# Gated attention on one core: two query blocks per load of K and V

## The chip, the cores and the metric

The kernel runs on one core of one Trainium2 chip. The metric is the device time of one execution in microseconds (us); several runs are taken and the median is given. A profile is one further execution, recorded instruction by instruction.

The core has five instruction streams. PE multiplies matrices (its weight loads, PEld, are listed apart). ACT evaluates functions such as exp. DVE and POOL do elementwise work and sums. SP issues most of the DMA transfers. PE writes to PSUM, the others read it; each stream runs its own instructions in order and waits on semaphores for the others.

## The reference

There are 2048 rows of width 512, and 32 heads of 128 channels with 2048 cached keys each. The output is an input plus attention times a gate.

```
x  = A_x;  xn = layernorm(x)
q  = (xn @ wq) as 32 heads of 128
p  = softmax(q @ k_cache^T * 128**-0.5)
s  = (p @ v_cache) @ wo
h  = relu(xn @ w1 + b1) ** 2           # 1792 wide
g  = silu(h @ w2 + b2)
out = x + s * g
```

## The kernel before

**Blocks, units, steps.** The 2048 query rows are cut into four blocks of 512 (`NQB`, `QB`). A unit `g` is one head for one block; before, unit `g` is block `g // 32`, head `g % 32`, so all heads of block 0 come first, then all of block 1, and so on: 128 units. A unit has eight steps (`NPR`), each for 256 keys; 1024 steps in all (`NPAIR`). In a step PE makes scores for two tiles of 128 keys (`gen_scores`, two matmuls of 512 columns into psA), ACT turns them into exponentials in one instruction of 128x1024 into one of eight buffers of pT, and PE, two steps later (`LAG`), multiplies the exponentials with V (`gen_pv`) into psO.

**Two ways for a unit.** Most units are "B" units (`gen_pv_b`): V is the stationary operand, 16 matmuls of 512 columns. The softmax denominators are then summed apart: POOL adds the halves of a pT tile into h_sum (`part_add`), DVE reduces it (`part_half`), or DVE reduces the pT tile alone (`den_part`); the sums go through DRAM (d_scr, r_scr) and come back spread over all partitions (r_all), and POOL scales the output into oT (`den_scale`). The units in `A_SET`, 20 of them, go the "A" way (`gen_pv`): the exponentials are stationary, V has a column of ones added, and 64 matmuls of 129 columns give output and denominators together. DVE copies them out (o_un), POOL scales (`norm_scale`), and a transposing DMA writes oT (`gen_oT`).

**K, V and weights.** K is loaded by two transposing DMAs and V by four plain ones per unit (`fill_k`, `fill_v`), into rings of three (`NSL`), two units ahead. `wq_sb` holds query weights per head in a ring of four. W1 and W2 stay in SBUF for the whole kernel (both are named w_sb in the profile). `wo_all` holds 16 heads of wo and is filled anew for every block.

**Projections.** In block 0, a head's Q is made from four matmuls of 512 columns (`job_proj`) and one cast by DVE to qt_sb. From block 1 on, heads come in pairs and are projected by seven products rather than eight (`job_pair`): 14 matmuls of 256 columns, whose stationary operands are sums of weight blocks made ahead (`wp_mul` on ACT, `wp_sums` on POOL, stored to wq_scr and loaded by `fill_pair`) and whose moving operands are sums of x blocks in xs_t (`x_sum` on POOL). DVE puts the seven results together (u_t and qt_sb, seven instructions of 128x256). The weights are scaled first by a power of two per head (`head_max`, `chunk_scale`).

**The gate and the output.** `job_h` makes h for a block, 14 chunks of four matmuls; DVE takes relu plus bias (r_t) and multiplies (h2T). `job_o2` makes 14 matmuls for each of four row tiles; tanh on ACT and two products on POOL give the gate in g_all. `job_wo` multiplies oT with wo in chunks of eight heads (the last of the last block has 16), and sums in acc; `acc_gate`, `acc_add` and `finish` apply the gate, add x and write out.

**The order.** A planner in Python writes the order of every engine by hand. `_Sched` keeps a modelled clock for each engine and `emit` adds an instruction with its waits. The main loop goes over the 1024 steps: scores of this step, then filler matmuls (`fill_one`: projections, h, o2, wo), then the values of two steps before. `credit` hands the fillers out evenly over the steps that are left; `soon` lets a filler in only if its inputs are ready by the modelled clock. Work for DVE, POOL and SP waits in lists (`quiet`, `pool_quiet`, `sync_quiet`) with due times. Before the loop the first head is written out by hand; its K is transposed by PE, and `fill_k(1)` waits for that (`t_kT0`). At the end a tail multiplies the last 16 heads with wo, 14 matmuls inside the loop and 22 (`n_after`) behind it, ahead of the ones that need the last head.

Nearly every instruction is made by a helper, so one line of the profile stands for many uses: 259 and 264 are matmuls, 268 ACT, 272, 277, 278, 282, 286 elementwise work, 327 the transposing sum, 335 and 339 plain and transposing DMAs.

Of the kernel before, what the change touches and what calls it, by code (L numbers as in the profile page):

```python
# [12 lines left out]
P = 128  # L13
# [48 lines left out]
def _cost(name, fn):  # L62
# [15 lines left out]
    if f in (_reduce_t, _abs_max):  # L78
        n = _elements(k["in_"])
    elif f is _reduce:  # L80
        n = _elements(k["in_"]) * 1.3 + 35
    elif f is _recip:
        n = n * 3.1
    elif f in (_bn_stats,):
        n = _elements(k["in_"])
    elif f is _ts and _in_sbuf(k["in0"]):
        n = n / 2
    elif f is _tt and k["out"].dtype == F16:
        n = n / 2
# [252 lines left out]
def bass_recurrent_scan__mha_block_cached__dense_activation_squared_relu__prompt_kernel(  # L342
# [17 lines left out]
    QB = 512  # L360
# [10 lines left out]
    SPB = H * NPR  # L371
    HC = 8
    NCH = H // HC
    CH = [[(m * HC, (m + 1) * HC) for m in range(NCH)] for _ in range(NQB - 1)]
    CH.append([(0, HC), (HC, 2 * HC), (2 * HC, H)])
# [9 lines left out]
    A_SET = (0, 10, 20, 28, 32, 36, 42, 44, 50, 60, 63, 72, 78, 84, 94, 102, 120, 125, 126, 127)  # L385
# [7 lines left out]
    NRW = 2 * HC  # L393
    WQ_PACE = 20
    WQ_FIRST = 64
    POOL_OWED = 1000
    HALF_SLACK = 300
    VW = 136

# [14 lines left out]
    NSL, NSW, NQS, NPT, NOT, NOC, NHS = 3, 4, 5, 8, 21, 5, 3  # L414
    xnT = sb("xnT", [P, NDC, 2 * QB], BF16)
    w1_sb = sb("w1_sb", [P, NDC, F], BF16)
# [4 lines left out]
    oT = sb("oT", [P, NOT, QB], BF16)  # L421
    acc = sb("acc", [P, TPB, D], F32)
# [10 lines left out]
    xs_t = sb("xs_t", [P, 4, 2, HB], F16)  # L433
# [23 lines left out]
    r_all = sb("r_all", [P, 2, QB], F32)  # L457
    d_scr = nc.dram_tensor("d_scr", [2, P, 32], F32, kind="Internal").ap()
# [43 lines left out]
    sl_xl = [S.slot(f"xl{i}") for i in range(TPB)]  # L502
    sl_xT = [S.slot(f"xT{i}") for i in range(TPB)]
    sl_w1 = [S.slot(f"w1{i}") for i in range(NFC // 2)]
# [20 lines left out]

    def is_b(g):
        assert g in b_no or g in a_no
        return g in b_no
# [17 lines left out]
    for i in [x for x in range(NSL) if at_a(x)]:  # L546
# [7 lines left out]
    t_xuse = {}  # L554
    n_xuse = [2] + [0] * (NQB - 1)
# [4 lines left out]

    def ln_x(jt):
        return x_t[:, jt - 2, :] if 2 <= jt < TPB else x_ln[:, jt % 2, :]

    def ln_y(jt):
        return out_t[:, jt - 2, :] if 2 <= jt < TPB else xn_t[:, jt % 2, :]

    def ln_prev(jt):
        return jt - TPB if jt < TPB + 2 else jt - 2

    def ln_load(j, i, eng=SP):  # L570
        jt = j * TPB + i
        assert jt < TPB or ln_prev(jt) in t_xn
        t_xl[jt] = S.emit_dma(
            eng, partial(_dma, out=ln_x(jt), in_=A_x[0, jt * P:(jt + 1) * P, :]), sl_xl[i],
# [24 lines left out]
    def ln_scale(j, i):  # L599
        jt = j * TPB + i  # L600
        assert jt < TPB or ln_prev(jt) in t_xnr
# [5 lines left out]
    def ln_transpose(j, i):  # L607
        jt = j * TPB + i
        t_xnr[jt] = tok_xT[j][i] = S.emit_dma(
            SP, partial(_dmaT, out=xnT[:, :, jt % (2 * TPB) * P:(jt % (2 * TPB) + 1) * P],  # L610
                        in_=ln_y(jt)),
            sl_xT[i], deps=[t_xn[jt], t_xuse.get(j - 2)])
        assert j < 2 or n_xuse[j - 2] == NFC + (H if j == 2 else NPP)

    def ln_next(j, i):
        ln_scale(j, i)
        ln_transpose(j, i)
        if i + 2 < TPB:
# [8 lines left out]
    def load_k0(b):  # L627
# [3 lines left out]
            SP, partial(_dma, out=kT[:, NSL - 1, b * n * P:(b + 1) * n * P],  # L631
# [14 lines left out]
    def k0_transpose(b):  # L646
        n = NKT // 2
        for c in range(n):
            t_kT0[b] = E(PE, partial(_peT, out=bankO(b).bitcast(BF16)[:, c * P:(c + 1) * P],
                                     in_=kT[:, NSL - 1, (b * n + c) * P:(b * n + c + 1) * P],  # L650
# [61 lines left out]
    t_kfill = [None] * NG  # L712
    t_vfill = [None] * NG
    t_wqfill = [None] * NG
# [13 lines left out]
    def fill_k(g, part=None):  # L728
        if g >= NG:
            return  # L730
        h, i, prev = g % H, g % NSL, g - NSL
        n = Sk // NKP
        for x in range(NKP) if part is None else [part]:
            t_kfill[g] = S.emit_dma(
                SP, partial(_dmaT, out=kT[:, i, x * n:(x + 1) * n],
                            in_=A_k_cache[0, h, x * n:(x + 1) * n, :]),
                sl_k[i], deps=[t_S_last[prev] if prev >= 0 else t_kT0[1]],
                group_done=x == NKP - 1)

    def fill_v(g, part=None):  # L740
        if g >= NG:
            return
        h, i, prev = g % H, g % NSL, g - NSL
        n = NKT // NVP
        dst = v_sb[:, i, :, 0:Dh] if at_a(g) else v_row[:, i]
        if part == 2 and at_a(g):
            t_ones[g] = E(GP, partial(_memset, out=v_sb[:, i, :, Dh:Dh + 1], val=1.0),
                          deps=[t_PV_last[prev]])
        for x in range(NVP) if part is None else [part]:
            t_vfill[g] = S.emit_dma(  # L750
# [3 lines left out]
                sl_v[i], deps=[t_PV_last[prev] if prev >= 0 else None],  # L754
                group_done=x == NVP - 1)

    def fill_wq(g, eng=SP):
        if g >= H:
            return
        h, i, prev = g % H, g % NSW, g - NSW  # L760
        t_wqfill[g] = S.emit_dma(
            eng, partial(_dma, out=wq_sb[:, i, :, :],
                        in_=A_wq[:, h * Dh:(h + 1) * Dh].rearrange("(c p) e -> p c e", p=P)),
            sl_wq[i], deps=[t_proj[prev], t_hm[prev]] if prev >= 0 else [])

    def wo_prev(j, i):
        h = i * HC + HC - 1
        return (j * H + h - NRW) if h >= NRW else (j - 1) * H + h + NRW

    def load_wo(j, i, x):  # L770
        n = HC // NWP
        h0 = i * HC + x * n
        prev = wo_prev(j, i)
        tok_wo[j, i] = S.emit_dma(
            SP, partial(_dma, out=wo_all[:, h0 % NRW:h0 % NRW + n, :], in_=wo_view[:, h0:h0 + n, :]),
            sl_wo[i % 2], deps=[t_wodone[prev]] if prev >= 0 else [], group_done=x == NWP - 1)
# [12 lines left out]
    t_xs = {0: None}  # L789
# [4 lines left out]
    def wp_load(p):  # L794
        t_wn[p] = S.emit_dma(
            SP, partial(_dma, out=wq_new[:, 0:2 * NDC * Dh].rearrange("p (c e) -> p c e", c=NDC),
                        in_=A_wq[:, 2 * p * Dh:(2 * p + 2) * Dh].rearrange("(c p) e -> p c e", p=P)),
            sl_wn, deps=[t_ws.get(p - 1)])
# [7 lines left out]

    def chunk_turn(q):
        t_mr[q] = E(DV, partial(_transpose32, out=mx_r[:], in_=mx_q[:]),
                    deps=list(t_hm.values()) + [t_mp.get(q - 1)])
# [1159 lines left out]
```

## Time and profile before

| | us |
|---|---|
| median of 3 runs (1211.37 to 1211.56) | 1211.52 |
| span of the profiled execution | 1210.6 |
| DMA: moved, mean rate | 235.79 MB, 195 GB/s |
| exponentials on ACT, 1025 instructions | 1028.6 |
| halves added on POOL (h_sum), 666 | 754.1 |
| DVE sums of h_sum, 666, and of pT, 198 | 442.8 and 238.3 |
| pair evictions on DVE: u_t, qt_sb, 144 each, at 0.458 and 0.465; 48 at 0.452 | 65.9, 66.9, 21.7 |
| relu on DVE (r_t), 56 at 0.723 | 40.5 |
| oT scaled on POOL, 108 at 1.283 | 138.5 |
| a DMA issued by POOL: 16 of x_t at 0.593 | 9.5 |

The span is the time from the first to the last recorded instruction of one execution. Busy times are unions over an engine's instructions, so a share of 99% means that the engine is hardly ever without an instruction; a matmul record includes the time that its result takes through the array, and records overlap. "x" gives the number of instructions, "<-" what a group writes and reads, and behind the bar stand the busy time and the mean time of one in ns, then idle time ahead of the group and what ended it.

### The profile page before, as it was taken

The numbers are of one execution on the slowest core, as the hardware profiler recorded it, in microseconds if no ns is written. First come the engines' busy times: TensorE is split into PE (matmuls) and PEld (weight loads), VectorE is DVE, ScalarE is ACT, GpSimd is POOL, SyncE is SP. The second block draws the span as 40 slices with busy tenths as digits, with TensorE's granted clock in tenths as the row PEclk, the third lists the DMA queues.
The fourth block names the chain that finished last, engine by engine and source line by source line (L and its number), as shares of the span: only waits on it lengthen the run. The fifth ranks groups of instructions, "written<-read, shape, count | busy, mean of one in ns | idle before, by whom it ended". The sixth has DMA issues, their size and how long they took to land.

```text
span 1210.6 us, 21032 instructions
## 1 busy us (share of the span) xinstructions
PE 1198.5 (99%) x6858; PEld 711.4 (59%) x6989; DVE 1076.3 (89%) x2037; ACT 1095.4 (90%) x1185; POOL 1078.1 (89%) x1035
## 2 busy tenths in 40 slices
PE   9999999999999999999999999999999999999999
PEld 7555555556665665555655656565565655555666
DVE  6999998998989987998799999978979999999873
ACT  7998999999999999999899899989999999999994
POOL 5998998999889888999899897979989899999873
PEclk9999999999999999999999999999999999999999
DMA  9889988999998999898968888986787887878972
GB/s 210 185 206 209 220 199 207 207 196 225 218 215 210 232 226 204 200 216 196 209 169 200 189 195 194 191 199 166 181 212 164 196 194 172 202 178 187 201 162 49
DMA packets 505821, 235.79 MB, mean 195 GB/s; under 512 B 394704, under 2 KB 482512, under 8 KB 505712
## 3 DMA queue, kind: packets, MB, share of 16 engines
q1 hardware_dynamic: 503616, 230.38, 84.8%
q0 software_dynamic: 1424, 3.81, 1.0%
q8 instruction: 55, 0.90, 0.3%
q14 instruction: 54, 0.44, 0.1%
q10 hardware_dynamic: 672, 0.26, 0.1%
HBM read 152.06 MB, written 11.49 MB: 135 GB/s over the span
## 4 chain that ended last, share of the span: by engine, by line
PE 90%; DVE 4%; POOL 3%; issue 1%; DMA 1%; ACT 1%; SPq 0%; POOLq 0%; ACTq 0%; DVEq 0%
PE psA L259 33%; PE psO L259 28%; PE psF L259 17%; PE psO L264 5%; PE psF L264 5%; POOL h_sum L272 2%; DVE d_part L327 2%; POOL oT L272 1%; DMA r_all<-r_scr 1%; DMA kT<-in_A_k_cache_dram 0%; DVE h2T L282 0%; DVE u_t L277 0%; ACT pT L268 0%; DVE r_t L278 0%; DVE qt_sb L282 0%
## 5 line engine op out<-in xcount | busy, mean ns | idle before, releaser
L268 ACT ACTIVATE pT<-psA 128x1024 bf16<-128x1024 f32 x1025 | 1028.6, 1025 | 95.1 <-PE psA L259 67.5
L272 POOL TENSOR_TENSOR h_sum<-pT 128x512 f32<-128x512 bf16 x666 | 754.1, 1158 | 47.9 <-ACT pT L268 34.7
L259 PE MATMUL psA<-qt_sb,kT 128*128 128x512 bf16 x1969 | 592.1, 380 | 4.0 <-ACT pT L268 0.3
L259 PE MATMUL psO<-pT,v_sb 128*128 128x512 bf16 x1683 | 504.2, 379 | 2.8 <-DVE o_un L286 0.3
L327 DVE TRANSPOSE_TENSOR_REDUCE d_part<-h_sum 128x16 f32<-128x512 f32 x666 | 442.8, 683 | 16.4 <-POOL h_sum L272 15.2
L259 PEld LDWEIGHTS psA<-qt_sb,kT 128*128 128x128 bf16 x2032 | 279.3, 145 | 166.0 <-ACT pT L268 8.3
L259 PEld LDWEIGHTS psO<-pT,v_sb 128*128 128x128 bf16 x1728 | 168.9, 98 | 152.8 <-issue 1.8
L327 DVE TRANSPOSE_TENSOR_REDUCE d_part<-pT 128x32 f32<-128x1024 bf16 x198 | 238.3, 1211 | 2.3 <-ACT pT L268 2.0
L259 PE MATMUL psF<-wo_all,oT 128*128 128x512 bf16 x468 | 153.1, 379 | 0.5
L272 POOL TENSOR_TENSOR oT<-o_col,r_all 128x512 bf16<-128x512 f32 x108 | 138.5, 1283 | 10.9 <-DMA r_all<-r_scr 10.7
L264 PEld LDWEIGHTS psO<-v_sb,pT 128*128 128x128 bf16 x1280 | 85.3, 98 | 30.8 <-issue 0.4
L264 PE MATMUL psO<-v_sb,pT 128*128 128x129 bf16 x1280 | 98.3, 220 | 0.1
L259 PE MATMUL psF<-w_sb,h2T 128*128 128x512 bf16 x220 | 73.1, 379 | 0.2
L259 PE MATMUL psF<-xnT,w_sb 128*128 128x512 bf16 x218 | 72.2, 379 | 0.3
L282 DVE SCALAR_TENSOR_TENSOR qt_sb<-psF,sc_q,u_t 128x256 bf16<-128x256 f32 x144 | 66.9, 465 | 5.1 <-PE psF L264 3.0
L277 DVE TENSOR_SCALAR u_t<-psF,sc_q 128x256 f32<-128x256 f32 x144 | 65.9, 458 | 6.1 <-PE psF L264 5.2
L259 PEld LDWEIGHTS psF<-wo_all,oT 128*128 128x128 bf16 x480 | 46.9, 98 | 41.2
L264 PE MATMUL psF<-xs_t,wq_sb 128*128 128x256 f16 x384 | 68.3, 273 | 0.0
L268 ACT ACTIVATE o_col<-psO 128x512 f32<-128x512 f32 x108 | 64.2, 594 | 0.0
L264 PEld LDWEIGHTS psF<-xs_t,wq_sb 128*128 128x128 f16 (+1 forms) x384 | 37.1, 98 | 29.2 <-DVE u_t L277 2.6
L264 PE MATMUL psF<-xnT,wq_sb 128*128 128x256 bf16 x288 | 54.2, 273 | 0.0
L272 POOL TENSOR_TENSOR wq_sb<-wq_sb 128x256 f16<-128x256 bf16 (+1 forms) x64 | 42.9, 673 | 11.5 <-ACT wq_sb L268 11.3
(86 smaller groups left out, 724.6 us busy)
## 6 DMA issues: line engine op xcount, KB each, us to landing
v_sb<-in_A_v_cache_dram SPq DMA_DIRECT2D x508, 128.0 KB, 2.9
r_all<-r_scr SPq DMA_DIRECT2D x108, 256.0 KB, 3.9
wq_sb<-wq_scr SPq DMA_DIRECT2D x48, 448.0 KB, 4.3
wo_all<-in_A_wo_dram SPq DMA_DIRECT2D x64, 256.0 KB, 3.4
wq_scr<-wq_sb SPq DMA_DIRECT2D x16, 448.0 KB, 3.7
wq_sb<-in_A_wq_dram SPq DMA_DIRECT2D x16, 256.0 KB, 4.3
kT<-in_A_k_cache_dram SPq DMA_TRANSPOSE x254, 3.9
wq_sb<-in_A_wq_dram SPq DMA_DIRECT2D x31, 128.0 KB, 3.1
```

Of the source, the lines that this page charges most:

```text
L259: return e.matmul(out, lhsT, rhs, start=start, stop=stop)
L264: return e.matmul(out, lhsT, rhs, start=start, stop=stop, skip_group_check=True)
L268: return e.activation(out, in_, func, bias=bias, scale=scale)
L272: return e.tensor_tensor(out, in0, in1, op)
L277: return e.tensor_scalar(out, in0, scalar1=scalar1, scalar2=None, op0=op0)
L282: return e.scalar_tensor_tensor(out=out, in0=in0, scalar=scalar, in1=in1, op0=op0, op1=op1)
L327: return e.tensor_reduce(out, in_, axis=AX.X, op=ALU.add, apply_transpose=True)
```

## The change

**Order of units.** Blocks are taken two at a time. For a pair of blocks, heads go two by two, and the units run (block a, head h), (block b, head h), (block a, head h+1), (block b, head h+1); the first and the last two heads of the whole run as (a, h), (a, h+1), (b, h), (b, h+1). `kv_of(g)` numbers the 64 loads of K and V, each used by two units; the rings have two places rather than three. K of head 0, transposed by PE, is now read through oT's memory, and the load of head 1 waits no more for its transposes.

```diff
+    for jj in range(NQB // 2):
+        for h in range(0, H, 2):
+            a, b = [(2 * jj, h), (2 * jj, h + 1)], [(2 * jj + 1, h), (2 * jj + 1, h + 1)]
+            ends = (jj, h) in ((0, 0), (NQB // 2 - 1, H - 2))
+            units += a + b if ends else [a[0], b[0], a[1], b[1]]
-    NSL, NSW, NQS, NPT, NOT, NOC, NHS = 3, 4, 5, 8, 21, 5, 3
+    NSL, NSW, NQS, NPT, NOC, NHS = 2, 4, 6, 8, 5, 3
-    A_SET = (0, 10, 20, 28, 32, 36, 42, 44, 50, 60, 63, 72, 78, 84, 94, 102, 120, 125, 126, 127)
+    A_SET = (0, 3, 6, 9, 13, 15, 19, 20, 26, 30, 32, 45, 50, 54, 62, 71, 75, 78, 101, 109, 118, 125, 126, 127)
```

**Block 1 early.** xnT holds all four blocks. The four row tiles of block 1 are loaded ahead of head 1's K, into memory that acc uses later, and normalised right behind the first head's hand-written part; blocks 2 and 3 come from step 138 on.

```diff
+    for i in range(TPB):
+        ln_load(1, i)
     fill_k(1)
-    fill_wq(2)
     fill_v(1)
...
+    for i in range(TPB):
+        ln_bn(1, i)
+        ln_rstd(1, i)
+    for i in range(TPB):
+        calm(1, partial(ln_next, 1, i))
```

**Projections.** Only heads 0 to 7 of blocks 0 and 1 are projected plainly: 16 units rather than 32, two of them in the hand-written start. All others go in pairs, 56 rather than 48. A pair's weights are loaded once for two blocks (28 loads of wq_scr). `PREP` sets the order in which weights are made ready: the maxima of heads 8 to 31 come from loads of their own (`pair_max`), and the weights of heads 0 to 7 are prepared late, for blocks 2 and 3. xs_t has a place for each of two blocks.

```diff
-    for g in range(2, H):
-        jobs.append((NPR * g - 15, NPR * (g - 2), job_proj(g), g))
-    for g in range(H, NG, 2):
-        jobs.append((NPR * g - 20, NPR * g - 26, job_pair(g), g))
+    for g in range(2, 4 * NPL):
+        jobs.append((NPR * g - 15, NPR * (g - 3), job_proj(g), ("q", g)))
     for j in range(NQB):
+        for p in range(NPL if j < 2 else 0, NPP):
+            g = un[j, 2 * p]
+            jobs.append((NPR * g - 40, NPR * g - 26, job_pair(j, p), ("pair", j, p)))
```

**W1, wo and gates.** W1 is streamed through three places of 256 columns, seven loads for each block. wo_all holds eight heads and is filled once for two blocks; its last chunk goes into W2's memory. The gates are written to DRAM (g_scr) by POOL's queue and loaded by SP when a block's output needs them. acc has eight row tiles.

```diff
+        def gate():
+            t = E(GP, partial(_tt, out=th_t[:, 0, :], in0=th_t[:, 0, :], in1=z_t[:, s, :],
+                              op=ALU.mult), deps=[box[0]])
+            t_gated[jt] = t_zrd[s] = t_thr[0] = E(
+                GP, partial(_tt, out=out_t[:, s, :], in0=th_t[:, 0, :], in1=z_t[:, s, :],
+                            op=ALU.add), deps=[t, t_outdma[s]])
+            t_gw[jt] = t_outdma[s] = S.emit_dma(
+                GP, partial(_dma, out=g_scr[jt], in_=out_t[:, s, :]), sl_out[s],
+                deps=[t_gated[jt]])
```

**Relu and the last sums.** The relu of h goes to ACT where the model has ACT idle, and otherwise stays on DVE. `finish` always runs on DVE and is used for blocks 2 and 3 only; for blocks 0 and 1 all four chunks are summed in acc, and `acc_add` writes the output tile.

```diff
-            t1 = E(DV, partial(_ts, out=r_t[:, s, :], in0=bankF(bank), scalar1=b1f[:, c:c + 1],
-                               scalar2=0.0, op0=ALU.add, op1=ALU.max),
-                   deps=[box[0], t_b1[0], t_rt[s]])
+            deps = [box[0], t_b1[0], t_rt[s]]
+            if AC.t <= PE.t + ACT_ROOM:
+                t1 = E(AC, partial(_act, out=r_t[:, s, :], in_=bankF(bank), func=ACT.Relu,
+                                   bias=b1f[:, c:c + 1]), deps=deps)
+            else:
+                t1 = E(DV, partial(_ts, out=r_t[:, s, :], in0=bankF(bank), scalar1=b1f[:, c:c + 1],
+                                   scalar2=0.0, op0=ALU.add, op1=ALU.max), deps=deps)
```

**The planner.** `job_needs` lists what each filler waits for. `crowded` holds back fillers without a due time while projections with a near one are outstanding, and `need_q`, called at the first step of a unit, places fillers until the unit's Q has been placed.

```diff
+    def crowded(n, step):
+        for key, rel, job, tag in jobs[:8]:
+            if deadline(tag) is not None:
+                n += job[0]
+                if deadline(tag) < step + 4 + n * 0.8:
+                    return True
+        return False
+
+    def need_q(g, step):
+        room = ROOM
+        while t_evac[g] is None:
+            if fill_one(step) or fill_one(step, any_job=True):
+                continue
...
+        if k == 0 and pi >= NPR:
+            need_q(g, pi)
         if pi >= NPR:
             gen_scores(pi)
```

**The end.** The last chunk has eight heads; block 2's last chunk (32 matmuls) and block 3's (the tail) run behind the last scores, block 2's first.

More of the change, by code (lines that the diff above doesn't have):

```diff
@@ L87, in _cost @@
         n = n / 2
-    elif f is _tt and k["out"].dtype == F16:
+    elif f is _tt and k["out"].dtype in (F16, BF16) and k["in0"].dtype in (F16, BF16):
         n = n / 2
@@ L524, in at_a, with wide @@
         return g in A_SET
+    def wide(kv):
+        return any(at_a(g) for g in range(NG) if kv_of(g) == kv)
     def is_b(g):
@@ L872, in wp_sums @@
+    def wp_sums(n, i):
         a, s = parts(wq_new)
[L873 to L877 removed]
```

721 lines of the change are left out of this document (418 added, 303 removed).

## Prediction

> **What bounds the kernel now.** I read four views in this order: the busy times and the chain of waits on the page, the stretches of 40 us, the waits of PE, and the time line of the end.
>
> ```profile
> span 1210.6 us, 21032 instructions
> PE 1198.5 (99%) x6858; PEld 711.4 (59%) x6989; DVE 1076.3 (89%) x2037; ACT 1095.4 (90%) x1185; POOL 1078.1 (89%) x1035
> PEclk9999999999999999999999999999999999999999
> PE 90%; DVE 4%; POOL 3%; issue 1%; DMA 1%; ACT 1%; SPq 0%; POOLq 0%; ACTq 0%; DVEq 0%
> ...
> L259 PE MATMUL psA<-qt_sb,kT 128*128 128x512 bf16 x1969 | 592.1, 380 | 4.0 <-ACT pT L268 0.3
> L264 PE MATMUL psO<-v_sb,pT 128*128 128x129 bf16 x1280 | 98.3, 220 | 0.1
> L264 PE MATMUL psF<-xs_t,wq_sb 128*128 128x256 f16 x384 | 68.3, 273 | 0.0
> ```
>
> PE is in use all the time and is nine tenths of the chain. The other three engines have 115 to 134 us of idle time each, so they matter only where they make PE wait.
>
> ```profile
> 0.00:40.00 40.00, 38.18 (x328) 26.89 (x332) 29.09 (x60) 31.26 (x34) 24.73 (x36) 1.00 1.06 208
> 40.00:80.00 40.00, 39.79 (x183) 21.33 (x186) 39.16 (x75) 36.95 (x40) 37.22 (x35) 1.00 0.82 185
> 480.00:520.00 40.00, 39.48 (x226) 23.58 (x228) 33.26 (x61) 38.15 (x43) 34.59 (x36) 1.00 0.95 212
> 800.00:840.00 40.00, 39.53 (x201) 22.57 (x203) 35.63 (x68) 36.54 (x41) 39.06 (x35) 1.00 0.86 209
> ```
>
> Columns are the stretch, its length, busy time and count of PE, PEld, DVE, ACT and POOL, granted clock, DMA share, GB/s. The second stretch has 186 weight loads, one for each matmul of 512 columns: 40/186 = 0.215 us from one to the next. I take 0.216. A matmul of 256 columns is 380 - 273 = 107 ns shorter, so 0.109 us; one of 129 columns 160 ns shorter, so 0.056 to 0.057 us. The time line gives the same: 16 of 129 columns in 1.07 us, whose last has 0.22 us of latency, 0.85/15 = 0.057.
>
> Now the budget. The weight loads are complete; 131 matmul records are missing (6989 - 6858), and each hole looks like 2 x 216 - 379 = 53 ns of idle time. The weight loads by group give 4824 of 512 columns, 688 of 256, 1280 of 129 and 195 of 128 (0.056): 1042.0 + 75.0 + 72.9 + 10.9 us, and 1.8 us because the first 36 run at half rate (4.02 us for 36). That is **1202.6 us of matmul issue in a span of 1210.6**. Of the 8 us left, 1.0 is ahead of the first matmul, 2.6 behind the last. Full stretches read 39.79 (four holes); what the stretches from 40 to 1200 lack of that adds up to 1.5 us, the largest being the 0.31 and 0.26 shown. The rest is in the first 16 us. So no wait worth more than 1.5 us is there to be removed in the body.
>
> ```profile
> PE psO L303 <- DMA kT<-in_A_k_cache_dram: 0.5, 1, 0.5
> ...
> 1195.11 1.07 PE L264 MATMUL psO<-v_sb,pT 128*128 128x129 bf16 x16
> 1197.12 3.40 PE L259 MATMUL psF<-wo_all,oT 128*128 128x512 bf16 x15
> ```
>
> The only wait of PE for a DMA is 0.5 us, at the start.
>
> **The change part by part.** *Traffic.* A unit's K and V are four loads of 128 KB and two of 256 KB, 1 MB; 64 of 128 go: -64 MB. wo is loaded 32 times, not 64, at 256 KB: -8. Pair weights 28, not 48, at 448 KB: -8.8. W1 28, not 7, at 256 KB: +5.3. Gates, 16 writes and 16 reads at 128 KB: +4. Net some -71 MB of 236. The DMA engines are at 0.82 to 1.06 in the stretches above, but PE waited for them 0.5 us in all: **0 us**. What hides it is PE's own queue of work. The SP queue is shorter too (a K half holds it 1.2 us), so what moves past it, pair weights and wo, comes no later.
>
> *Projections.* 14 plain ones stay in the stream where there were 30: 64 fewer matmuls of 512, -13.8 us. Eight more pairs: 112 matmuls of 256, +12.2. **-1.6 us.**
>
> *Heads.* 24 heads, not 20, go the A way: four times (64 x 0.057 - 16 x 0.216) = 4 x 0.19 = **+0.8 us**. Other engines: four B heads take 32 denominators with them (by the shares of the 666 and 198: -28.6 us on POOL, -25.8 on DVE), 4 x 1.05 of sums, turns and reciprocals on DVE, 4 x 1.28 on POOL; four A heads give back 4.1 and 4.2.
>
> *Other engines' ledger.* A pair's evictions are seven instructions, 3 x 0.458 + 3 x 0.465 + 0.452 = 3.2 us of DVE; eight more are +25.8, less 16 casts at 0.62 = -9.9. The last sums all go to DVE (+7 x 1.26), accumulator adds +12 x 0.67, last products -8 x 0.67. DVE comes out at about +1 us if each relu stays there and -40 (56 x 0.723) if ACT takes all, which has 115 us idle. POOL: 16 gate stores issued, 16 x 0.59 = +9.4; four more sums of x, +4.7; 14 finishes fewer, -17.8; with the heads -33. **0 us** on PE; without that cover POOL's 33 us would still be a gain, and DVE's +1 is paid in a margin of 134.
>
> *Start.* Unit 2 is now block 1 of head 0, so the second block's normalisation moves from 110-205 us into the first 27. Scores of unit 1 start at 17.05 us and unit 2's came at 26.5 before. DVE is through its share of block 0 at about 15.7; four statistics (0.66 + 0.16) end at 19.0; the four transposes hold SP 1.21 us each from about 19.4, the last issued at 23.1 and landed 2.4 to 3.3 us later, 25.5 to 26.4; four matmuls 0.9, a cast 0.7: unit 2's Q at 27.1 to 28.0. Queued behind that wait on PE are unit 2's scores, behind them ACT's exponentials and the last two value steps of unit 1. Ahead of it the builder may place W1 matmuls (three buffers, six chunks, 24 matmuls, 5.2 us), so what is surely exposed is the cast, some 0.9 us with its signals. Four loads of x (0.47 us each on SP) go ahead of K of head 1, but its wait for the first K transposes, which held SP till 7.5, goes away: K landed at 13.98 and is needed at 17.05, so it stays in time. Bounds: -0.8 us (some of the start's gaps close) to +4.0 (few matmuls placed ahead). The nearest rows are in the lower half: **+1.2 us.**
>
> *Body.* Waits already there: -1.5 if all go, +8 if new ones come; the order is made by the same kind of planner, whose misses were 1.5 us: **-0.4 us**.
>
> *End.* A last chunk of eight heads, not sixteen, leaves 30 wo matmuls of block 2 and seven of block 3 between the last value step and the last head's output (37 x 0.216 = 8.0 us, before 22, `n_after`, x 0.216 = 4.8), against some 5 us from eviction to landed transpose. **0 us.**
>
> Sum: 1210.6 - 1.6 + 0.8 + 1.2 - 0.4 = 1210.6 of span. The median shown is 0.9 above the profiled span, so **1211.5 us: no change that can be told**. I count a change as visible from 0.2% (2.4 us), about what a measurement of this kernel can tell.
>
> **The rivals.** *Faster*, below 1209.1: with every body wait gone and no cost at the start, 1211.5 - 1.2 - 1.1 = 1209.2, with the start's gaps closing too 1208.4 down to 1207.8. For it: 71 MB less traffic and 33 us less POOL. Against it: PE hardly waited for either. 0.22.
>
> *Slower by the start.* The place is unit 2's Q. It decides if the W1 matmuls placed ahead run out more than 2 us before Q lands: the builder holds them back while a Q due soon is outstanding (`crowded`), and the real transposes may land after the modelled ones. 3 us late plus the cast gives 1214.5; a stall that let the rate fall as at the start (36 matmuls at 0.106 instead of 0.056) would add 1.8: 1216.3. 0.16. The Trainium skill, "TensorE: Matmul & The Clock Gate", Part 1, says that the clock falls to half after an idle window of about 3.4 us; the half rate of the first 36 is what the trace has of that, and no stall of that length stands in it.
>
> *Slower by POOL and DVE*, early: eight sums of x (9.3 us) and four small normalisation steps (3.0) enter POOL in the first 70 us, where DVE is at 39.16 of 40. Against it: six of the first 16 units are A heads, not two. If relief and load don't meet, half of the 12 us, 6, reaches PE through the eight buffers of pT: 1217.5, bounds 4 to 10. 0.16.
>
> *Relu with a table load.* The page has one ACT_TABLE_LOAD (1.28 us) for Exp, Tanh and Copy. If Relu needed two at each of 56 places, 144 us would meet ACT's 115 idle: up to 1272. 0.02. The Trainium skill, "ScalarE: Activation LUTs", section on table sets, says that relu is in every set; by that nothing is loaded, and no run so far shows it. The same page's rules for kernel authors would keep relu on VectorE; by rows it is 0.72 there and 0.59 for a copy of that size on ACT.
>
> **How the numbers follow.** Chances: no change 0.44, faster 0.22, slower 0.16 + 0.16 + 0.02 = 0.34. The likeliest case's own range is 1209.1 to 1213.9. The range of 8 in 10 reaches from 1207.8 to the upper bound of the POOL case, 1211.5 + 10 = 1221.5, and leaves out the table loads and the worst ends of the start's and POOL's cases, 2 in 10 together.
>
> **What would show it.** Weight loads of 512, 256 and 129 columns at 4704, 792 and 1536; the strides unchanged; DMA share about 0.3 lower with PE's busy share still 99%; the scores of unit 2 between 26.5 and 29 us; one table load; behind the last value step no hole in PE. Wrong would be: an idle stretch of PE over 2 us anywhere behind 30 us, exponentials that wait for denominators, or a span under 1208.2, which the matmuls and the 2.6 us of the end hardly allow.

## The result, and the profile after

| | before | after |
|---|---|---|
| median of 6 runs each (lowest to highest), us | 1211.69 (1211.37 to 1211.89) | 1216.10 (1215.65 to 1216.39) |
| span of the profiled execution, us | 1210.6 | 1213.8 |
| DMA moved, mean rate | 235.79 MB, 195 GB/s | 160.15 MB, 132 GB/s |
| share of 16 DMA engines, the hardware queue | 84.8% | 53.1% |

The ratio is 1.0035, 95% interval 1.0023 to 1.0047. The changed kernel is slower by 4.4 us, which is more than the 0.2% that the prediction took for what can be told. The time lies inside the predicted range, but the forecast, no change, did not come. Rows of the changed kernel's page that were shown of before too, and three stretches of 40 us:

```profile
span 1213.8 us, 20930 instructions
PE 1198.9 (99%) x7077; PEld 720.9 (59%) x7213; DVE 1077.2 (89%) x2048; ACT 1092.9 (90%) x1184; POOL 1056.4 (87%) x1028
PE 98%; issue 1%; ACT 1%; DVE 1%; POOL 0%; DVEq 0%; POOLq 0%
L264 PE MATMUL psO<-v_sb,pT 128*128 128x129 bf16 x1536 | 118.2, 220 | 0.0
L264 PE MATMUL psF<-xs_t,wq_sb 128*128 128x256 f16 x448 | 79.5, 273 | 0.1
```

```profile
0.00:40.00 40.00, 36.44 (x318) 24.52 (x322) 30.06 (x67) 28.29 (x31) 22.56 (x40) 1.00 0.78 165
40.00:80.00 40.00, 39.71 (x270) 24.20 (x274) 36.98 (x70) 35.69 (x38) 30.72 (x29) 1.00 0.88 188
800.00:840.00 40.00, 39.79 (x196) 22.70 (x199) 36.90 (x70) 37.02 (x40) 39.24 (x36) 1.00 0.44 106
```

PE still is in use nearly all the time, the clock is 1.00, and the matmuls have the forecast counts (4704, 792 and 1536 of 512, 256 and 129 columns) and spacings. The DMA share fell as said; 75.6 MB fewer are moved (the prediction's 71 counts a KB as 1024 bytes and a MB as 1024 KB). What stands out is the first stretch: 36.44 us of PE, where it was 38.18. The waits of PE name what it waited for (total, times, longest):

```profile
PE psA L259 <- DVE qt_sb L286: 1.3, 1, 1.3
PE psA L259 <- POOL mhalf L294: 1.0, 1, 1.0
PE psF L259 <- DVE h2T L282: 0.8, 1, 0.8
```

The middle one is the 1.0 us ahead of the first matmul, which both kernels have. The other two are new. (This view counts from the end of a matmul's record, which includes its time through the array, so its 0.8 and 1.3 are the 0.95 and 1.46 below.)

**Where the 4 us are.** I took the start of every matmul in the trace, and from each interval to the next start its own stride (216 ns for 512 columns, 109 for 256, 56.6 for 129); what is left is time in which PE issued nothing. Records missing from a trace blur this by some tenths, so the table uses two traces that have all of them: the kernel before with 26 unused semaphores added, and the changed kernel with 16 semaphores fewer. Both keep the order of PE, ACT, DVE and POOL and the time of the kernel that they stand for (they are the first two experiments).

| us | before | after | difference |
|---|---|---|---|
| PE without issue, 0 to 16 us | 3.98 | 3.66 | -0.3 |
| 16 to 35 us | 0.01 | 2.56 | **+2.55** |
| 35 to 1180 us | 1.37 | 2.39 | +1.0 |
| 1180 us to the last matmul | 0.10 | 0.35 | +0.25 |
| from the last matmul to the end of the span | 2.61 | 3.87 | **+1.26** |
| the rest: matmul issue and the 1.0 ahead of it | 1201.7 | 1200.7 | -1.0 |
| span | 1209.8 | 1213.6 | +3.8 |

The stretch from 16 to 35 us and the end make up 3.8 us, as much as the whole; what the body loses (+1.0) the shorter matmul issue gives back (-1.0). The time outside the span, run by run, is 1.8 us before and 2.1 after, another 0.3.

**The start.** The time line of the changed kernel between 24.7 and 31 us, rows of DVE, one of ACT, then PE's (start, length, engine, line, operation, what it writes and reads, count, idle time before and what ended it):

```profile
26.54 1.62 DVE L282 SCALAR_TENSOR_TENSOR h2T<-psF,b1f,r_t 128x512 bf16<-128x512 f32 x2 [0.59 <-ACT r_t L268]
29.21 0.75 DVE L282 SCALAR_TENSOR_TENSOR h2T<-psF,b1f,r_t 128x512 bf16<-128x512 f32 x1 [0.47 <-ACT r_t L268]
29.88 0.68 DVE L286 CAST qt_sb<-psF 128x512 bf16<-128x512 f32 x1
...
28.49 0.69 ACT L268 ACTIVATE r_t<-psF,b1f 128x512 bf16<-128x512 f32 x1 [1.13 <-PE psF L259]
...
24.75 1.89 PE L259 MATMUL psF<-xnT,w_sb 128*128 128x512 bf16 x7
27.43 1.02 PE L259 MATMUL psF<-xnT,w_sb 128*128 128x512 bf16 x4 [0.79 <-DVE h2T L282]
28.29 1.03 PE L259 MATMUL psF<-xnT,wq_sb 128*128 128x512 bf16 x4
30.62 0.60 PE L259 MATMUL psA<-qt_sb,kT 128*128 128x512 bf16 x2 [1.30 <-DVE qt_sb L286]
```

The last transpose of block 1 had landed at 26.79. The planner put three W1 chunks, twelve matmuls one behind another, ahead of unit 2's Q (one of the twelve is missing from the record). There are two banks of psF, and each is free only when ACT's relu (0.69) and, after it, DVE's second step (0.75) have read it: PE makes a chunk in 0.86 us, but 0.95 is lost at 26.3 to a bank. Then come Q's own four matmuls, at 28.29, 1.5 us after the landing, and the cast, on DVE behind the last such step; 1.46 us is lost there. Unit 2's scores start at 30.62 (before: 26.66). A plan that puts Q's matmuls right behind the landing was not run.

**The end.** PE's and DVE's rows in the changed kernel, whose last matmul ended at 1209.95, and behind the dots the last ones of the kernel before:

```profile
1206.72 3.22 PE L259 MATMUL psA<-w_sb,oT 128*128 128x512 bf16 x30
1209.55 0.42 DVE L272 TENSOR_TENSOR z_t<-psA,g_all 128x256 f32<-128x256 f32 x1
1210.00 0.42 DVE L272 TENSOR_TENSOR x_t<-z_t,acc 128x256 bf16<-128x256 f32 x1
1210.53 0.29 DVE L272 TENSOR_TENSOR z_t<-psA,g_all 128x128 f32<-128x128 f32 x1
1211.58 0.29 DVE L272 TENSOR_TENSOR x_t<-z_t,acc 128x128 bf16<-128x128 f32 x1
...
1206.83 1.11 PE L259 MATMUL psA<-wo_all,oT 128*128 128x128 bf16 x17
1207.98 0.29 DVE L272 TENSOR_TENSOR z_t<-psA,g_all 128x128 f32<-128x128 f32 x1 [0.18 <-PE psA L259]
1208.31 0.29 DVE L272 TENSOR_TENSOR x_t<-z_t,acc 128x128 bf16<-128x128 f32 x1
```

The last row tile is cut into 256, 128 and 128 columns. With eight heads rather than sixteen, PE delivers these 0.87, 0.45 and 0.45 us apart, half of before. DVE needs a product and a sum for each, 1.0, 0.7 and 0.6 us, and has hardly a break till 1211.87, 1.92 us behind PE. Before, DVE waited for PE there, and its last sum ended at 1208.60, 0.66 behind a last matmul that ended at 1207.94. 1.92 - 0.66 = 1.26, all of the difference.

### The profile page after: what moved, and what is told of

The parts are those of the page before. It is cut to its first block, busy times and chain, and to the rows that moved or that the text cites. A ratio compares the mean times of both kernels' runs of the same rounds, so it can differ in the third digit from the quotient of the medians.

```text
span 1213.8 us, 20930 instructions
## 1 busy us (share of the span) xinstructions
PE 1198.9 (99%) x7077; PEld 720.9 (59%) x7213; DVE 1077.2 (89%) x2048; ACT 1092.9 (90%) x1184; POOL 1056.4 (87%) x1028
## 2 busy tenths in 40 slices
DMA packets 334891, 160.15 MB, mean 132 GB/s; under 512 B 249888, under 2 KB 314144, under 8 KB 334784
## 3 DMA queue, kind: packets, MB, share of 16 engines
q1 hardware_dynamic: 331920, 152.64, 53.1%
## 4 chain that ended last, share of the span: by engine, by line
PE 98%; issue 1%; ACT 1%; DVE 1%; POOL 0%; DVEq 0%; POOLq 0%
PE psA L259 36%; PE psO L259 29%; PE psF L259 18%; PE psO L264 7%; PE psF L264 7%; ACT pT L268 0%; PE psA L264 0%; ACT o_col L268 0%; DVE x_t L272 0%; DVE z_t L272 0%; DVE h2T L282 0%; PE psO L303 0%; ACT r_t L268 0%; PE psF L303 0%; DVE qt_sb L282 0%
## 5 line engine op out<-in xcount | busy, mean ns | idle before, releaser
L272 POOL TENSOR_TENSOR h_sum<-pT 128x512 f32<-128x512 bf16 x650 | 736.1, 1159 | 69.6 <-ACT pT L268 42.5
L259 PE MATMUL psO<-pT,v_sb 128*128 128x512 bf16 x1626 | 486.7, 379 | 2.3
L327 DVE TRANSPOSE_TENSOR_REDUCE d_part<-h_sum 128x16 f32<-128x512 f32 x650 | 433.7, 685 | 21.8 <-POOL h_sum L272 20.1
L327 DVE TRANSPOSE_TENSOR_REDUCE d_part<-pT 128x32 f32<-128x1024 bf16 x182 | 219.1, 1209 | 2.4 <-ACT pT L268 2.2
L264 PEld LDWEIGHTS psO<-v_sb,pT 128*128 128x128 bf16 x1536 | 102.4, 98 | 31.5 <-DVE o_un L286 0.3
L264 PE MATMUL psO<-v_sb,pT 128*128 128x129 bf16 x1536 | 118.2, 220 | 0.0
L282 DVE SCALAR_TENSOR_TENSOR qt_sb<-psF,sc_q,u_t 128x256 bf16<-128x256 f32 x168 | 78.6, 468 | 9.8 <-PE psF L264 7.1
L277 DVE TENSOR_SCALAR u_t<-psF,sc_q 128x256 f32<-128x256 f32 x168 | 77.1, 459 | 11.4 <-PE psF L264 11.0
L264 PE MATMUL psF<-xs_t,wq_sb 128*128 128x256 f16 x448 | 79.5, 273 | 0.1
L264 PEld LDWEIGHTS psF<-xs_t,wq_sb 128*128 128x128 f16 x448 | 43.5, 98 | 32.9 <-DVE u_t L277 2.7
```

The lines of the kernel that those rows point to most:

```text
L259: return e.matmul(out, lhsT, rhs, start=start, stop=stop)
L264: return e.matmul(out, lhsT, rhs, start=start, stop=stop, skip_group_check=True)
L272: return e.tensor_tensor(out, in0, in1, op)
L277: return e.tensor_scalar(out, in0, scalar1=scalar1, scalar2=None, op0=op0)
L282: return e.scalar_tensor_tensor(out=out, in0=in0, scalar=scalar, in1=in1, op0=op0, op1=op1)
L327: return e.tensor_reduce(out, in_, axis=AX.X, op=ALU.add, apply_transpose=True)
```

## The experiments

My theory: the start (2.55) and the end (1.26) each have one cause on the chip, and traffic has none. Rivals: the number of semaphores, traffic, and the order that the planner makes. Edits are against the changed kernel unless "before" is said, and ratios are to the kernel before, whose median beside these runs was 1211.9 to 1212.5.

**Semaphores.** The changed kernel has more of them.

```diff
+    for i in range(26):
+        S.slot(f"spare{i}")
```

> The kernel before, with 26 semaphores that nothing uses, as many as the change has more than before (92 against 66). Theory (the time outside the span, 1.0 us before and 2.1 after, grows with the semaphores of the program, some 0.042 us each): span as before, 1210.6, time 1212.8. Rival (it grows with something else of the change, such as the gates' buffer in DRAM or POOL's 16 more transfers): time 1211.7, span 1210.6.

Measured: 1211.67 (1211.30 to 1213.11, 10 runs), ratio 0.9993 (0.9984 to 1.0003), span 1209.8. The other way round, in the changed kernel:

```diff
-    sl_xl = [S.slot(f"xl{i}") for i in range(NQB * TPB)]
-    sl_xT = [S.slot(f"xT{i}") for i in range(NQB * TPB)]
+    sl_xl = [S.slot(f"xl{i}") for i in range(2 * TPB)]
+    sl_xT = [S.slot(f"xT{i}") for i in range(2 * TPB)]
```

> The changed kernel, with 16 semaphores fewer: the loads of x and the transposes of row tiles 8 to 15 use those of tiles 0 to 7. Same order of instructions. Theory of the semaphores: span 1213.8, time outside it 1.4 instead of 2.1, so 1215.4. Rival: no difference, 1216.1.

Measured: 1215.85 (1215.69 to 1216.77, 7 runs), ratio 1.0031 (1.0020 to 1.0042), span 1213.6. Both theories of the semaphores fell: they cost nothing that shows, and they are not the 0.3 us outside the span either, which stays at 1.8 and 2.1 (the 1.0 that the first expectation gives for before took a span and times from different executions).

**The start: take the wait away.** Q of units 2 and 3 from block 0's rows, so that nothing waits for block 1's normalisation. This run and the next two also carry two small changes of the planner that are not shown here (when a pair's maxima count as done, and fillers placed until the last use of an output buffer has been planned); what these do alone was not measured.

```diff
-        js = slice(j * QB, (j + 1) * QB)
+        jx = 0 if g < 4 else j
+        js = slice(jx * QB, (jx + 1) * QB)
...
-                  deps=[t_wqfill[h], t_bankF[bank]] + tok_xT[j], inc=(n == NDC - 1))
+                  deps=[t_wqfill[h], t_bankF[bank]] + tok_xT[jx], inc=(n == NDC - 1))
```

> The changed kernel, with the Q of units 2 and 3 projected from block 0's rows instead of block 1's, so nothing waits for block 1's normalisation there (the rows of block 1 for heads 0 and 1 are then not the reference's). Theory (the two PE holes at 26.3 and 28.9 us, 0.95 and 1.46, come from placing twelve W1 matmuls and then unit 2's Q at the last moment): both holes go, PE's idle time before 35 us falls by 2.0 to 2.4, the time to 1213.7 to 1214.1. Rival (DVE and POOL are behind by the early normalisation itself, whoever waits for it): holes of the same sum show up within the next 30 us, and the time stays above 1215.5.

Measured: 1220.51 (1220.49 to 1220.67, 4 runs), ratio 1.0067 (1.0052 to 1.0082), span 1218.7. From 16 to 35 us PE lost 0.01 us, so the wait was gone; but from 35 to 1180 it lost some 9.4, where the changed kernel has 2.4, and the end took 4.29. Neither expectation held in full: the idle time came back, and more than that, but spread over the run and not within 30 us. The planner works from its modelled clocks: after the first 215 weight loads PE's order is another one, and the A units had been chosen for the old order. So the same edit once more, with A units chosen anew for the new order and the last row tile in two pieces:

> As e2 (Q of units 2 and 3 from block 0's rows, so the rows of block 1 for heads 0 and 1 are not the reference's), with the last tile in two pieces and a set of 22 A units chosen by the planner's own clock for this order. Theory (e2's new waits behind 35 us belong to an order that its A units were not chosen for; the wait for block 1 at the start costs 2.4 us): no hole from 16 to 35 us, PE's idle time from 35 to 1180 us near the changed kernel's 2.8 and not e2's 8.9, span 1210.6 to 1211.4, time 1213.0 to 1213.8. Rival (taking the wait away only moves it): the sum of PE's idle time stays above 8.5 us, the time above 1215.

Measured: 1216.06 (1215.63 to 1216.57, 5 runs), ratio 1.0034 (1.0020 to 1.0048), span 1213.9. The start is free (0.01), the end 3.53, and the body loses 5.75, in pieces of 0.86, 0.68, 0.62 and 0.61 us at 912, 1111, 326 and 808 us and smaller ones. The rival held: what the start gives, this order takes back elsewhere. These two runs therefore don't show what the wait alone costs.

**The start: normalise earlier.** The statistics and scales of block 1 are interleaved, the next W1 load goes behind the transposes, and 18 A units are chosen anew (the end is in two pieces here too).

```diff
-    for i in range(TPB):
-        calm(1, partial(ln_next, 1, i))
+        if i:
+            ln_next(1, i - 1)
+    ln_next(1, TPB - 1)
```

> The changed kernel with block 1's normalisation drawn forward (each row tile scaled and its transpose issued as soon as the next one's statistics are placed, ahead of the next W1 load), the last row tile in two pieces instead of three, and another set of 18 A units, chosen by the planner's own clock, because the order of the body is made anew. Theory (start and end are most of the loss): PE's idle time from 16 to 35 us falls from 2.6 to under 1.2, from the last matmul to the end 3.4 instead of 3.87, six A units fewer save 6 x 0.19 of matmuls; span some 1.5 us under 1213.8, time near 1214.6. Rival (the body's waits answer for the loss): the start and the end gain, but the span stays within 0.5 of 1213.8.

Measured: 1218.10 (1216.96 to 1218.73, 4 runs), ratio 1.0050 (1.0035 to 1.0065), span 1215.2. The wait of PE in that run:

```profile
PE psO L259 <- DVE o_un L286: 3.5, 2, 3.1
```

DVE's queue runs in order. With the normalisation ahead of it, the copy that frees unit 0's output (o_un) came at 21.65 rather than at 18.54, and PE stood 3.24 us at 18.8. The wait moved; it did not go. The body of this order, another one again, has gaps of up to 0.86 us.

**The start: shorten one step.** DVE's second step for six chunks of h works on 32 columns, in the order of the changed kernel.

```diff
+            if j == 0 and c < 6:
+                DV.prog[-1] = (DV.prog[-1][0], partial(
+                    _stt, out=h2T[:, c, 0:32], in0=bankF(bank)[:, 0:32], scalar=b1f[:, c:c + 1],
+                    in1=r_t[:, s, 0:32], op0=ALU.add, op1=ALU.mult), DV.prog[-1][2])
```

> The changed kernel with the order of every engine kept, in which DVE's second step for the first six chunks of h of block 0 (h2T) works on 32 of 512 columns (0.75 us becomes some 0.1), and the gate of block 0 reads six other chunks in their place. Theory, PE's two stretches at 26 and 30 us are DVE's queue: a bank of psF is free only when ACT's relu and DVE's step have both read it, and the cast of unit 2's Q stands behind the last such step. Then the first stretch falls from 0.95 to 0.4 or less, the second from 1.46 to 1.0 or less, idle time of PE from 16 to 35 us from 2.57 to 1.5 or less, span 1212.2 to 1213.0, us 1214.3 to 1215.1. Rival, the four transposes of block 1 land late (26.79) and set both stretches: they stay, 2.3 or more, us 1215.7 to 1216.4.

Measured: 1214.98 (1214.74 to 1215.65, 9 runs), ratio 1.0025 (1.0015 to 1.0035), span 1212.6. The same rows of its time line:

```profile
28.64 0.25 DVE L282 SCALAR_TENSOR_TENSOR h2T<-psF,b1f,r_t 128x32 bf16<-128x32 f32 x1 [0.47 <-ACT r_t L268]
28.81 0.68 DVE L286 CAST qt_sb<-psF 128x512 bf16<-128x512 f32 x1
...
26.86 1.02 PE L259 MATMUL psF<-xnT,w_sb 128*128 128x512 bf16 x4 [0.29 <-DVE h2T L282]
29.55 0.60 PE L259 MATMUL psA<-qt_sb,kT 128*128 128x512 bf16 x2 [0.80 <-DVE qt_sb L286]
```

The two stretches fell from 0.95 and 1.46 to 0.45 and 0.96, and the idle time from 2.57 to 1.57. The first stretch and the sum miss the theory's bounds by 0.05 and 0.07 (a step of 32 columns still took 0.25 us and not 0.1), and the sum is far from the rival's 2.3. Scores of unit 2 start 1.07 us earlier, with the transposes as they were (the last landed at 26.69): in this order the two readers of a bank and DVE's queue hold Q, not the transposes. The 1.57 us that are left were not taken away by any run that keeps the order.

**The end.** First, POOL takes every second of the last sums, as in the kernel before.

```diff
-        eng = DV
+        eng = DV if s else GP
```

> The changed kernel, with the last sum of the even row tiles on POOL again and only the odd ones on DVE. Theory (the end is bound by DVE, which does both the product and the sum of every tile while PE delivers a tile each 1.73 us): from the last matmul to the end of the span goes from 3.87 us back to about 2.6, the span from 1213.8 to 1212.6, the time from 1216.1 to 1214.9. Rival (the end is bound by the output's transfers, which the tighter spacing of the tiles crowds): the 3.87 stay within 0.3 and the time stays at 1216.1.

Measured: 1217.65 (1216.84 to 1218.48, 4 runs), ratio 1.0043 (1.0028 to 1.0058); the end grew to 4.94 us. My theory of that run fell. The time line of DVE, then of POOL:

```profile
1207.15 1.55 DVE L272 TENSOR_TENSOR out_t<-z_t,acc 128x512 bf16<-128x512 f32 x1
1209.67 1.26 DVE L272 TENSOR_TENSOR x_t<-z_t,acc 128x256 bf16<-128x256 f32 x1
...
1206.89 1.26 POOL L272 TENSOR_TENSOR out_t<-z_t,acc 128x512 bf16<-128x512 f32 x1 [1.76 <-DMA out_dram<-out_t]
1209.38 1.26 POOL L272 TENSOR_TENSOR x_t<-z_t,acc 128x512 bf16<-128x512 f32 x1 [1.23 <-DVE z_t L272]
```

Beside a sum on POOL, DVE's sum takes 1.55 us for 512 columns and 1.26 for 256, where it takes 0.69 and 0.42 alone; each ends 0.3 to 0.55 us behind POOL's. So help from POOL cost more than it gave. Next, the last row tile in two pieces, which spares DVE a product and a sum:

```diff
-    cuts = [0, D // 2, 3 * D // 4, D]
+    cuts = [0, D // 2, D]
```

> The changed kernel, with the last row tile's columns in two pieces (256, 256) instead of three (256, 128, 128); nothing else. Theory (behind the last matmul DVE still has the last tile's work: 0.42 twice and 0.29 four times, 2.3 us with gaps, against 1.77 of matmuls): from the last matmul to the end 3.4 instead of 3.87, time -0.4. Rival (the output's transfers bind, and a larger last piece lands later): 3.87 or more.

Measured: 1215.38 (1215.25 to 1216.21, 6 runs), ratio 1.0028 (1.0017 to 1.0040), span 1213.2, end 3.53. The theory held, 0.1 short of its 3.4. And the products left out:

```diff
+                if j == 3:
+                    finish(jt, c0, c1, box[0], place)
+                    return t_fin[jt]
```

> The changed kernel, without the products by the gate in the last chunk of block 3 (six DVE instructions; the sum reads the eight heads straight from psF and psA, so the last chunk's share of these 512 rows goes in without its gate). Theory, the end is late because DVE's product and sum for each tile, 0.69 + 0.69, do not fit the halved spacing of the tiles with what is queued: from the last matmul to the end of the span 2.4 to 2.9 us rather than 3.87, span 1212.2 to 1212.9, us 1214.3 to 1215.0. Rival, the end is late for another reason (the output's store, or the sum's wait for acc): 3.4 or more, us 1215.6 to 1216.2.

Measured: 1214.80 (1214.38 to 1215.51, 10 runs), ratio 1.0022 (1.0013 to 1.0032), span 1212.6, end 2.46. DVE's last row is

```profile
1210.15 0.29 DVE L272 TENSOR_TENSOR x_t<-psA,acc 128x128 bf16<-128x128 f32 x1 [0.15 <-PE psA L259]
```

0.33 us behind a last matmul that ended at 1210.11, and now it waits for PE. With half of DVE's work gone, the lag is gone, and the rival with it.

**Traffic.** First, 62 MB were given back to the changed kernel: behind every K and V load from the third head on, SP issues a copy of the same rows from DRAM to DRAM, with no wait on it before the end.

```diff
+    def again(x, kv, r0, r1, src):
+        SP.prog.append(([], partial(_dma, out=more[x, kv, r0:r1, :], in_=src[0, kv % H, r0:r1, :]),
+                        ("dma", sl_more.sem)))
+        sl_more.val += 16
...
+            if kv > 1:
+                again(0, kv, x * n, (x + 1) * n, A_k_cache)
```

> The changed kernel, with the traffic of K and V that it saves given back: behind each load of K or V for heads from the third load on, one more transfer of the same bytes from the same place goes to a scratch in DRAM, on SP's queue; the planner's order stays as it is. Theory (the traffic was hidden and is worth nothing): DMA share up by 0.15 or more, time within 0.5 us of the changed kernel's 1216.1. Rival (less traffic is already a gain that other losses hide): 1 us slower or more, with waits for r_all, pair weights or K in POOL's and PE's lists.

Measured: 1241.85 (1239.57 to 1248.31, 4 runs), ratio 1.0255 (1.0226 to 1.0284), span 1240.5. "Traffic is worth nothing" fails here by 26 us, but this run is a poor test of it: the kernel before carries 236 MB and has no such waits, while here 372 issues are put into a hand-made order of SP that does not know them. A copy also reads and writes its bytes in DRAM: by the page 172 MB were read and 79 written, in the changed kernel 107 and 14, in the kernel before 152 and 11. Two more took the two apart: copies of 16 rows, and copies of 512 KB.

> The changed kernel, with the same 372 copies behind the K and V loads on SP's queue, each of 16 rows (4 KB) rather than 128 or 256 KB, so 1.5 MB in all. Queue theory (the copies cost 26 us because each holds SP some 0.5 us in an order that does not know them): at least half of the 26 us stays, 1229 to 1242, and r_all is waited for. Bandwidth theory (the bytes of a copy cost, read and written): below 1218, span 1213.5 to 1216.

> The changed kernel, with the same bytes copied (62 MB read and 62 MB written) by 124 issues of 512 KB, one behind the last K load and one behind the last V load of a head, rather than 372. Queue theory: a third of the issues, so about 1216.1 + 26/3 = 1225 or less. Bandwidth theory: 1236 or more, since a packet behind 512 KB waits longer, not less.

Measured: the tiny ones 1228.76 (1227.44 to 1229.23, 4 runs), ratio 1.0133 (1.0118 to 1.0148), with only 1.6 MB more moved than in the changed kernel; the large ones 1231.18 (1230.00 to 1232.05, 4 runs), ratio 1.0154 (1.0139 to 1.0169). Neither theory held alone: the tiny copies miss the queue theory's 1229 by 0.2, and the large ones lie between the two theories. Of the 26 us, 12.7 come with the issues alone, and 124 issues with all the bytes cost 15.1. In the run of tiny copies what SP delayed is seen in the waits:

```profile
POOL oT L272 <- DMA r_all<-r_scr: 26.2, 20, 2.9
```

where the changed kernel has 6.2 us. What copies cost in this order of SP is thus known, but not yet what the loads of before were worth. So the question was put to the kernel before. Leaving out the K and V loads of units 5, 7, 9 and so on:

```diff
+        if g > 4 and g % 2:
+            t_kfill[g] = t_S_last[prev]
+            return
```

> The kernel before, with the K and V loads of units 5, 7, 9, ... 127 left out (62 MB of 236; those units work on the rows that lie in their buffers, so their heads are wrong, and nothing else is left out). Theory, traffic is worth nothing where PE does not wait for it: 1211.7 within 0.8, span 1209.6 to 1210.4, DMA share from 0.85 to about 0.6. Rival, traffic has a price all over the body (as the 26 us of the copies added to the changed kernel would have it): 1200 or less is excluded by the matmul issue of 1202.6, so a gain down to the floor, span 1208.5 or less, us 1210.5 or less.

Measured: 1214.39 (1214.26 to 1214.78, 10 runs), ratio 1.0020 (1.0010 to 1.0029), span 1212.8: slower with less to move, which neither theory had. The planner counts SP's time, and without the loads it wrote another order: PE's differs after its first 1657 weight loads, and has a new gap of 1.56 us at 953 us and smaller ones. The last run keeps the plan and swaps only the finished instructions:

```diff
+            if g > 4 and g % 2:
+                SP.prog[-1] = (SP.prog[-1][0], partial(
+                    _dmaT, out=kT[:, i, x * n:x * n + P],
+                    in_=A_k_cache[0, h, x * n:x * n + P, :]), SP.prog[-1][2])
```

> The kernel before, with its plan and the order of every engine kept, and the K and V loads of units 5, 7, 9, ... 127 cut to an eighth of their bytes (128 of 1024 rows of a K half, 16 of 128 partitions of a V quarter; those units work on what lies in their buffers): 54 MB less, the same count of issues. Theory, traffic is worth nothing to PE, and run e9 lost its 2.5 us by the order that the planner made anew: 1211.7 within 0.6, span 1209.3 to 1210.3. Rival, bytes have a price all over the body of the kernel before: span 1208.8 or less, us 1210.6 or less.

Measured: 1211.56 (1211.30 to 1211.93, 11 runs), ratio 0.9994 (0.9985 to 1.0003). Its page:

```profile
span 1209.7 us, 21032 instructions
DMA packets 362909, 178.91 MB, mean 148 GB/s; under 512 B 278224, under 2 KB 339600, under 8 KB 362800
q1 hardware_dynamic: 360704, 173.50, 61.3%
```

57 MB fewer move, the queue's share falls from 84.8% to 61.3%, and the time is that of before. Theory held, rival fell: bytes taken away were worth nothing to this kernel, as long as the issues and the order stay.

No version here beats the kernel before. Nor does one follow from the sum: 1213.6 less 2.55 and 1.26 is 1209.8, the span of before, so even a free start and the old end would only draw level.

## Why the prediction was wrong

**The start: the term that failed most.** The prediction gave +1.2 us: the W1 matmuls placed ahead ("24 matmuls, 5.2 us") would hide the wait at PE's own pace, and "what is surely exposed is the cast, some 0.9 us with its signals". Unit 2's Q was to be there at 27.1 to 28.0 and its scores between 26.5 and 29; the cast ended at 30.56, and the scores began at 30.62. The transposes came nearly as worked out (25.5 to 26.4 forecast for the last one, 26.79 measured). But twelve W1 matmuls were placed, not 24, and they run at the pace of the two engines that empty psF, 0.69 + 0.75 us and signals for each bank; the last of these steps stands ahead of the cast in DVE's queue. 2.55 us came: inside the bounds of -0.8 to +4.0, at the upper part. With DVE's step cut to a third, the second stretch was 0.96, which is the exposed cast. The rival "slower by the start" had the right place and about the right delay, with another cause: neither stretch stands where W1 matmuls had run out before a transpose, the first waits for a bank and the second for the cast.

**The end: 0 us, wrong by 1.26.** The step looked at the 37 matmuls that cover the last head's output, and that cover held (PE lost 0.35 us there). It did not look at what a chunk of eight heads does to DVE: pieces arrive in half the time, while the product and the sum of each stay as they were, and all sums had gone to DVE. The 7 sums were in the ledger as busy time, "0 us on PE"; at the end no PE work covers them. (The 1.26 us that the ledger gives for each is what a sum took beside one on POOL; alone it takes 0.69.)

**The body: -0.4 forecast, +1.0 measured**, within its bounds. No piece is larger than 0.31 us, and which waits these are stays open. That such gaps come and go with the planner's order is seen in three runs with another order: the two with Q from block 0's rows, and the kernel before without half of its loads, lost some 7.0, 3.4 and 3.0 us more in the body than the kernels that they started from.

**Projections and heads: -0.8 forecast, -1.0 measured** for the matmul issue, right. **Traffic, 0 us:** right, as far as the kernel before with small loads shows it. **Relu:** one table load of 1.28 us, as before. The Trainium skill, "ScalarE: Activation LUTs", section on table sets, has relu in every set; the trace agrees. But ACT took 3 of the 56 only, those of the three chunks at the start, so DVE's relief did not come (1077.2 us, before 1076.3): the +1 case of the ledger. POOL's busy time fell by 21.7 us, not 33: of the 32 denominators' sums that go with four heads, 16 were POOL's (666 to 650), not 25. **POOL and DVE early**: no exponential waited for POOL's sums in the first 400 us (in the whole run it is 1.5 us, before 0.5), and the two stretches above are not of that kind.

**Span and median.** The prediction set the median 0.9 us above the span, from one execution's span and other executions' times. In each of the runs the difference is 1.8 before and 2.1 after. The profiled execution of before was some 0.8 us longer than the same order's later ones (1209.7 and 1209.8), which hid the error in the sum but not the 0.3 us, whose cause stays open: the three variants of the changed kernel that have another order (Q from block 0's rows, twice, and the early normalisation) have 1.8 again.

Together: +1.35 for the start (2.55 less 1.2), +1.26 for the end, +1.4 for the body, -0.2 for the rest of the table, +0.3 outside the span: 4.1, so 1215.6. The variant whose trace the table uses has a median of 1215.85, the changed kernel 1216.10.

## What to carry to other kernels

In this kernel PE has hardly any slack, and saved traffic and relieved engines were worth nothing to it; what decided were the two ends of the run, where less work covers. Count there, piece by piece, each engine that must finish behind the last matmul, at the new spacing. A filler covers a wait only as fast as its buffer comes free, so cost it by the readers of that buffer, one after the other, and not by PE. In a kernel whose order a planner writes, an edit that the planner sees tests the new order as well as the edit; change the finished instructions and keep the order if the cost of one thing is wanted.

## What the runs showed of the hardware

**A sum on DVE is held up beside a sum on POOL.** Sums of two SBUF operands take 0.69 us on DVE alone and 1.55 beside one on POOL (1.26 in the kernel before). DVE's product of PSUM with SBUF kept its 0.42 within a sum of POOL. The rows of the kernel before:

```profile
1203.39 1.26 DVE L272 TENSOR_TENSOR out_t<-z_t,acc 128x512 bf16<-128x512 f32 x1
1206.19 0.42 DVE L272 TENSOR_TENSOR z_t<-psA,g_all 128x256 f32<-128x256 f32 x1 [0.94 <-PE psA L259]
...
1202.84 1.27 POOL L272 TENSOR_TENSOR out_t<-z_t,acc 128x512 bf16<-128x512 f32 x1 [9.19 <-DVE z_t L272]
1205.33 1.27 POOL L272 TENSOR_TENSOR x_t<-z_t,acc 128x512 bf16<-128x512 f32 x1 [1.23 <-DVE z_t L272]
```

The Trainium skill, "SBUF — State Buffer", section "Who interferes with whom", says that a DVE instruction with two SBUF inputs contends with a GpSimd (POOL) instruction that reads SBUF, and calls the ports that the two share an exclusive lock. The trace agrees in the main: in the run with sums on POOL, POOL's kept its 1.26 and ended at 1206.89 + 1.26 = 1208.15, and DVE's, which had started at 1207.15, ended 0.55 us later, less than the 0.69 that it takes alone.

**Copies put into SP's order cost by their issues and by their bytes:** 372 tiny copies 12.7 us, 124 large ones 15.1, 372 of 128 and 256 KB 25.8. POOL's waits for r_all, which SP issues behind such copies, are 26.2, 18.8 and 31.7 us in these runs, against 6.2; that they are the whole of the cost is not shown.
